# Weights of the first seven chunks decoded half a chunk at a time in one bank of PSUM

## The chip, the cores and the metric

The kernel runs on one core of a Trainium2 chip, whose engines run at the same time and each take their own instructions in order: TensorE (PE in the profile; PEld is its loading of weights), VectorE (DVE), ScalarE (ACT), GpSimd (POOL) and SyncE (SP), which here only starts transfers. A queued instruction that waits holds up whatever stands behind it on its engine. SBUF and PSUM are the two memories beside the engines; PSUM has eight banks of 512 fp32 columns by 128 partitions. The metric is the device time in microseconds of one execution.

## The reference, cut to what matters

All inputs come as float64. One layer of attention with a memory term is followed by two wide layers:

```
scores = q @ k.T / sqrt(D), causal;  a = softmax(scores);  local = a @ v
q_p = elu(q) + 1;  mem = (q_p @ M_prev) / (q_p @ z_prev + 1e-6)
x = sigmoid(beta) * mem + (1 - sigmoid(beta)) * local     # 4 batches x 576 tokens, 8 heads x 64 = 512 columns
x = elu(x @ w_in) @ w_out                                 # w_in 512 x 2048, w_out 2048 x 512
out = leaky(x @ w2_in) @ w2_out                           # leaky(h) = max(0.01 h, h)
```

The wide layers are computed with split operands: a number is a high part in the chip's fp32r type and a low part, number minus high part, and three matmuls stand for one product.

## The kernel before, in words

**Weights.** A wide layer's 2048 inner columns are 16 chunks. A chunk has 128 of them: a 128x512 block of `w_in` and one of `w_out`. `load_w` reads both as pairs of 32-bit words (low word `lw`, high word `hw`) into `wraw`, a tile with two buffers, and builds the fp32 number from bits, 1024 columns per instruction: ACT copies `hw` scaled by 2^-112 into the SBUF tile `wm` (L110); DVE shifts it left by three (L111), ors in the top three bits of `lw` (L112) and the sign (L115); ACT casts the result to the high part in `w` (L226, in `copy`); POOL subtracts the high part to get the low part, 512 columns at a time (L121). Other chunks than the first seven are decoded late, in the wide layers.

**Attention.** Batches are worked one after the other, each as four pairs of heads, each pair as items of 256 or 320 tokens. An item goes PE scores into a bank `sc` (L411 in batch 0, L413 and L414 later), DVE scale, mask and maximum (L416), ACT exponential (L421), POOL and DVE the reciprocal of the sums (L430, L431), POOL scaling (L436), PE transposes into a bank `tp` (L442), ACT copies (L447, L232), PE the product with the values (L509). Batch 0 takes plain fp32 matmuls and puts that product into banks `pm`; later batches use split operands and the single bank `po`, first written by the transposes of `qp_unit` (L315). Batch 0 thus never touches `po`.

**Order.** The seven chunks of the first layer (`dec`) are handed out during batch 0, one each time a planned cost has passed (`DSPAN`); the first layer's seven chunks are used from the end of batch 0 on, when `phase1_units` of a finished batch fill PE between attention items. The order on each engine is then set by a scheduler that goes by its own estimate of durations. When batch 0 is done, `close_decode` gives the tiles of decoding back.

**PSUM.** The eight banks: `pm` two, `sc` three, `tp` two, `po` one.

Of the kernel before, what the change touches and what calls it, by code (L numbers as in the profile page):

```python
# [10 lines left out]
I32 = mybir.dt.int32  # L11
AF = mybir.ActivationFunctionType
ALU = mybir.AluOpType
# [6 lines left out]
def _f(ap):  # L20
    return ap.bitcast(F32)
# [3 lines left out]
def kernel(  # L25
# [14 lines left out]
    nc = tc.nc  # L40
# [16 lines left out]
    E_GH, E_WH, E_VH, E_MS, E_V32, E_XH, E_RS, E_Y = "V", "A", "V", "P", "P", "A", "P", "A"  # L57
# [34 lines left out]
    def load_w(key, pool, src_i, src_o, f, slot):  # L92

        w = pool.tile([P, 2, 2, DM], F32R, tag=f"w{slot}", name=f"w{slot}")
        wi_tiles[key, f] = w[:, :, 0].rearrange("p t (c n) -> p t c n", c=NKC)
        wo_tiles[key, f] = w[:, :, 1]  # L100
        raw = pools["wst"].tile([P, 2, DM, 2], I32, tag="wraw", bufs=2, name="wraw")
        nc.sync.dma_start(
            raw[:, 0].rearrange("p (c n) t -> p c (n t)", c=NKC),
            src_i[:, f * 2 * P:(f + 1) * 2 * P].rearrange("(c p) n -> p c n", p=P),
        )
        nc.sync.dma_start(raw[:, 1].rearrange("p n t -> p (n t)"), src_o[f * P:(f + 1) * P, :])
        rw = raw.rearrange("p a n t -> p (a n) t")
        lw, hw = rw[:, :, 0], rw[:, :, 1]
        m = pools["wst"].tile([P, 2 * DM], I32, tag="wm", bufs=pools["nwm"], name="wm")
        nc.scalar.activation(out=_f(m), in_=_f(hw), func=AF.Copy, scale=2.0 ** -112)  # L110
        nc.vector.tensor_scalar(out=m, in0=m, scalar1=3, scalar2=None, op0=ALU.logical_shift_left)  # L111
        nc.vector.scalar_tensor_tensor(  # L112
            out=m, in0=lw, scalar=29, in1=m, op0=ALU.logical_shift_right, op1=ALU.bitwise_or
        )
        nc.vector.scalar_tensor_tensor(  # L115
            out=m, in0=hw, scalar=-(1 << 31), in1=m, op0=ALU.bitwise_and, op1=ALU.bitwise_or
        )
        t = _f(m).rearrange("p (a n) -> p a n", a=2)
        copy(E_WH, w[:, 0], t)
        for a in range(2):  # L120
            nc.gpsimd.tensor_tensor(out=w[:, 1, a], in0=t[:, a], in1=_f(w)[:, 0, a], op=ALU.subtract)  # L121
# [10 lines left out]
    def halves(n):  # L132
# [20 lines left out]
        out=mask[:, 448:576], in_=mask[:, 448:576], pattern=[[-1, 128]], compare_op=ALU.is_ge,  # L153
        fill=-1e30, base=0, channel_multiplier=1,
    )
    wst_a = tc.tile_pool(name="wst_a", bufs=1, side="left")
    pools = {"wst": wst_a.__enter__(), "nwm": 2}

    ones = []
    for par in range(NR):  # L160
# [30 lines left out]
    def bank(tag):  # L191
        return psum.tile([P, 512], F32, tag=tag, bufs=BANKS[tag], name=tag)
# [31 lines left out]
    def copy(eng, dst, src):  # L224
        if eng == "A":
            nc.scalar.copy(dst, src)  # L226
        else:
            (nc.vector if eng == "V" else nc.gpsimd).tensor_copy(dst, src)  # L228
# [476 lines left out]

    def close_decode():
        wst_a.__exit__(None, None, None)
        pools["outer"] = tc.tile_pool(name="mlpx", bufs=1, reuse_waits="tile", side="left")
        early = pools["outer"].__enter__()
        for tag in ("x", "y", "xh0", "xl0"):  # L710
            pools["own", tag] = early
        pools["own"] = tc.tile_pool(name="mlp", bufs=1, reuse_waits="tile", side="left")
        pools["mlp"] = pools["own"].__enter__()
# [17 lines left out]
    c_mlp = NFA * 24 * NT / 2.4  # L731
    rate = (c_mlp - RESERVE) / (c_att - DELAY)
    dec = [lambda f=f: load_w(0, wpa, w1i, w1o, f, f) for f in range(NFA)]
    fill = []
    credit = pos = 0.0
    for c, u, done in att:
        u()
        pos += c
        while dec and pos >= c0 * DSPAN * (NFA - len(dec)) / NFA:
            with tc.high_priority(offset=0):  # L740
                dec.pop(0)()
        if done == 0:
            close_decode()
        if done is not None:
            fill += [(pos + DELAY, c2, u2) for c2, u2 in phase1_units(done)]
        if fill and fill[0][0] <= pos:
            credit += c * rate
        while fill and fill[0][0] <= pos and fill[0][1] <= credit:
            _, c2, u2 = fill.pop(0)
            credit -= c2  # L750
            with tc.high_priority(offset=FILL_OFF):
                u2()
# [8 lines left out]


    wun = [(1, lambda f=f: load_w(0, wpb, w1i, w1o, f, f - NFA)) for f in range(NFA, NF)]
    tail = True
    merge(side, wun[:NPRE])
    wun = wun[NPRE:]
    w2 = [lambda f=f: load_w(1, wpa, w2i, w2o, f, f) for f in range(NFA)]
    w2 += [lambda f=f: load_w(1, wpb, w2i, w2o, f, f - NFA) for f in range(NFA, NF)]
    def recut(dst, scr, t0, n):
# [136 lines left out]
```

## Time and profile before

| what | value |
|---|---|
| median of 3 runs | 1123.6 us (1121.98 to 1123.76) |
| the profiled execution, its own time | 1123.19 us |
| its span in the trace | 1121.4 us |
| busy PE, PEld | 1066.8 us (95%), 917.1 us (82%) |
| busy DVE, ACT, POOL | 600.0 us, 493.9 us, 599.9 us |
| share of the chain that ended last: PE, POOL, DVE | 69%, 7%, 6% |

A busy share is a mean over stages with different limits. Batch 0's attention fills the first 126 us or so, attention with the first layer's chunks between goes on to about 560 us, and the rest is wide layers alone, where PE is busy without a break. The page's line of 40 slices of 28 us shows the first stage apart: PE 6, 9, 7, 9 tenths, POOL 8, 8, 9, 7.

### The profile page before, as it was taken

What the parts mean: (1) busy time and instruction counts of PE and PEld (TensorE: products, weight loads), DVE (VectorE), ACT (ScalarE), POOL (GpSimd) and SP (SyncE); (2) the same over time, 40 slices, a digit from 0 to 9 for tenths busy, and PEclk for the clock granted to TensorE, in tenths of its full rate; (3) what the DMA queues carried; (4) which work ended last, traced back from release to release, by engine and by line L of the source; (5) the groups of instructions that cost most, each with busy time, mean ns of one, the idle gap of its engine ahead of it and who ended that gap; (6) DMA issues with size and microseconds to landing.
All of it is one profiled execution on the core that took longest, in us unless ns stands there. A gap on an engine that the chain in (4) does not pass through costs nothing.

```text
span 1121.4 us, 17423 instructions
## 1 busy us (share of the span) xinstructions
PE 1066.8 (95%) x5904; PEld 917.1 (82%) x5904; DVE 600.0 (54%) x1363; ACT 493.9 (44%) x1191; POOL 599.9 (53%) x724
## 2 busy tenths in 40 slices
PE   6979899999989999989999999999999999999997
PEld 3657799989989999868777888988888888888886
DVE  6865887788878856646666222656221232131132
ACT  6867787687877634543544223433111111111110
POOL 8897695585658634955865324755422322322222
PEclk9989999999999999989999999999999999999999
DMA  7633443563365228552646122341100110010010
GB/s 187 183 98 89 118 102 102 119 170 92 79 145 157 61 60 260 170 171 94 194 125 200 34 67 76 117 141 63 50 26 1 23 53 1 1 38 1 1 38 19
DMA packets 145912, 104.43 MB, mean 93 GB/s; under 512 B 81440, under 2 KB 139808, under 8 KB 145824
## 3 DMA queue, kind: packets, MB, share of 16 engines
q1 hardware_dynamic: 145824, 103.33, 32.1%
q8 instruction: 47, 0.77, 0.3%
q14 instruction: 41, 0.34, 0.1%
HBM read 73.80 MB, written 25.95 MB: 89 GB/s over the span
## 4 chain that ended last, share of the span: by engine, by line
PE 69%; DMA 9%; POOL 7%; DVE 6%; ACT 4%; issue 4%; SPq 2%; DVEq 0%; POOLq 0%; ACTq 0%
PE pm L603 16%; PE sc L854 14%; PE tp L603 12%; PE sc L631 5%; PE po L854 4%; PE pm L631 4%; PE po L509 3%; PE tp L442 3%; POOL w L121 2%; DMA x<-xq 2%; PE po L631 2%; PE pm L509 2%; DMA wraw<-in_moe_w_out_dram 1%; PE sc L413 1%; PE sc L414 1%
## 5 line engine op out<-in xcount | busy, mean ns | idle before, releaser
L610 POOL TENSOR_TENSOR gl<-e,gh 128x512 fp32r<-128x512 f32 (+2 forms) x181 | 202.0, 1119 | 348.7 <-DVE gh L228 304.3
L603 PE MATMUL tp<-xw,w 128*128 128x512 f32 (+1 forms) x504 | 147.0, 374 | 5.5 <-DVE e L617 5.5
L603 PE MATMUL pm<-xw,w 128*128 128x512 f32 (+1 forms) x496 | 143.8, 371 | 0.0
L854 PE MATMUL sc<-w,gh 128*128 128x512 f32 x448 | 137.7, 393 | 0.0
L436 POOL TENSOR_SCALAR pt<-pt,rs,omg 128x128 f32<-128x128 f32 (+4 forms) x160 | 107.2, 679 | 19.4 <-DVE rs L431 15.8
L631 PE MATMUL sc<-gh,w 128*128 128x512 f32 (+2 forms) x438 | 106.8, 344 | 5.7 <-DVE gh L228 3.2
L603 PEld LDWEIGHTS tp<-xw,w 128*128 128x128 f32 x504 | 92.2, 190 | 24.3 <-DVE e L617 6.0
L121 POOL TENSOR_TENSOR w<-wm,w 128x512 fp32r<-128x512 f32 x64 | 87.5, 1387 | 37.3 <-ACT w L226 37.1
L603 PEld LDWEIGHTS pm<-xw,w 128*128 128x128 f32 x496 | 90.5, 188 | 18.4
L421 ACT ACTIVATE pt<-pt,mx 128x128 f32<-128x128 f32 (+4 forms) x160 | 93.4, 585 | 23.4 <-DVE mx L416 21.7
L854 PEld LDWEIGHTS sc<-w,gh 128*128 128x128 f32 x448 | 83.1, 188 | 17.9
L603 PE MATMUL tp<-xv,w 128*128 128x512 f32 (+1 forms) x252 | 93.9, 373 | 0.0
L603 PE MATMUL pm<-xv,w 128*128 128x512 f32 (+1 forms) x248 | 92.0, 371 | 0.0
L631 PEld LDWEIGHTS sc<-gh,w 128*128 128x128 f32 x438 | 74.3, 188 | 18.2 <-DVE gh L228 4.6
L622 ACT ACTIVATE e<-pm 128x512 f32<-128x512 f32 (+1 forms) x40 | 22.2, 554 | 151.2 <-PE pm L603 151.1
L228 DVE CAST gh<-e 128x512 fp32r<-128x512 f32 (+2 forms) x146 | 76.5, 527 | 20.4 <-PE po L631 7.5
L442 PE MATMUL tp<-ident,pt 128*128 128x128 f32 x480 | 79.3, 277 | 8.3 <-ACT ah L232 3.2
L854 PE MATMUL sc<-w,gl 128*128 128x512 f32 x224 | 85.4, 393 | 0.0
L623 DVE TENSOR_TENSOR e<-tp,e 128x512 f32<-128x512 f32 (+1 forms) x40 | 25.4, 636 | 108.1 <-ACT e L622 108.1
L623 DVE TENSOR_TENSOR e<-pm,e 128x512 f32<-128x512 f32 (+1 forms) x40 | 25.5, 636 | 106.7 <-ACT e L622 106.6
L603 PE MATMUL pm<-xh,w 128*128 128x288 f32 x368 | 80.1, 303 | 2.1 <-ACT xh L226 1.7
L416 DVE CUSTOM_DVE_ANT_0 pt<-sc,mask 128x128 f32<-128x128 f32 (+4 forms) x160 | 69.0, 448 | 12.1 <-PE tp L442 6.0
(149 smaller groups left out, 2466.6 us busy)
## 6 DMA issues: line engine op xcount, KB each, us to landing
wraw<-in_moe_w_in_dram SPq DMA_DIRECT2D x32, 512.0 KB, 4.1
wraw<-in_moe_w_out_dram SPq DMA_DIRECT2D x32, 512.0 KB, 5.2
ys<-st SPq DMA_DIRECT2D x32, 144.0 KB, 3.3
x1s<-st SPq DMA_DIRECT2D x36, 128.0 KB, 1.8
x<-x1s SPq DMA_DIRECT2D x9, 512.0 KB, 3.6
out_dram<-st SPq DMA_DIRECT2D x36, 128.0 KB, 1.7
vn<-in_v_dram SPq DMA_DIRECT2D x64, 64.0 KB, 2.4
xq<-xp SPq DMA_DIRECT2D x24, 160.0 KB, 1.9
```

Of the source, the lines that this page charges most:

```text
L121: nc.gpsimd.tensor_tensor(out=w[:, 1, a], in0=t[:, a], in1=_f(w)[:, 0, a], op=ALU.subtract)
L228: (nc.vector if eng == "V" else nc.gpsimd).tensor_copy(dst, src)
L416: nc.vector.tensor_tensor_reduce(out=pt[0:m, k0:k0 + n], in0=sc[0:m, 0:n], in1=mk, op0=ALU.add, op1=ALU.min, scale=-0.125, scalar=mx[0:m, ...
L421: nc.scalar.activation(out=pt[0:m, 0:nk], in_=pt[0:m, 0:nk], func=AF.Exp, scale=-1.0, bias=mx[0:m, last:last + 1], accum_out=self.pd["ss"] ...
L436: nc.gpsimd.tensor_scalar(out=pt, in0=pt, scalar1=rs[0:m, i:i + 1], scalar2=omg[0:m, h:h + 1], op0=ALU.mult, op1=ALU.mult,)
L442: nc.tensor.transpose(dst, self.p[c][:, k0:k0 + kn], ident)
L509: nc.tensor.matmul(po[:, a:b], w, x, start=i == 0, stop=i == len(mms) - 1)
L603: nc.tensor.matmul(ph, wi[:, wj, kc, :], xx[:, kc, :], start=n_mm == 0, stop=n_mm == 11)
L610: nc.gpsimd.tensor_tensor(out=gl, in0=g, in1=_f(gh), op=ALU.subtract)
L623: nc.vector.tensor_tensor(out=t, in0=ph, in1=t, op=ALU.max)
L631: nc.tensor.matmul(py, wo[:, wj, ec * P:(ec + 1) * P], gg, start=opens and f == first and n_mm == 0, stop=closes and f == last and n_mm == 2,)
L854: nc.tensor.matmul(pos[tb], gg[:, tb * P:(tb + 1) * P], wo[:, wj, :], start=f == 0 and n_mm == 0, stop=f == NF - 1 and n_mm == 2,)
```

## The change

For the first seven chunks a chunk is decoded as two halves, `w_in` and then `w_out`, of 512 columns. [...] There is one bank `po`, so a half begins when the half before it has been subtracted. The two tiles `wm` of the first pool go away. After batch 0 the old code runs, for all other chunks.

```diff
         nc.sync.dma_start(raw[:, 1].rearrange("p n t -> p (n t)"), src_o[f * P:(f + 1) * P, :])
+        if pools["decode_bank"]:
+            for a in range(2):
+                lw, hw = raw[:, a, :, 0], raw[:, a, :, 1]
+                t = bank(pools["decode_bank"])
+                m = t.bitcast(I32)
+                nc.scalar.activation(out=t, in_=_f(hw), func=AF.Copy, scale=2.0 ** -112)
+                nc.vector.tensor_scalar(out=m, in0=m, scalar1=3, scalar2=None, op0=ALU.logical_shift_left)
+                nc.vector.scalar_tensor_tensor(
+                    out=m, in0=lw, scalar=29, in1=m, op0=ALU.logical_shift_right, op1=ALU.bitwise_or
+                )
+                nc.vector.scalar_tensor_tensor(
+                    out=m, in0=hw, scalar=-(1 << 31), in1=m, op0=ALU.bitwise_and, op1=ALU.bitwise_or
+                )
+                copy(E_WH, w[:, 0, a], t)
+                nc.vector.tensor_tensor(out=w[:, 1, a], in0=t, in1=_f(w)[:, 0, a], op=ALU.subtract)
+            return
...
-    pools = {"wst": wst_a.__enter__(), "nwm": 2}
+    pools = {"wst": wst_a.__enter__(), "nwm": 2, "decode_bank": "po"}
...
         wst_a.__exit__(None, None, None)
+        pools["decode_bank"] = None
```

The scheduler places everything anew. On ACT, before, the first decode stands behind the exponentials of the first item (L421; `pt` is an item's scores, `w0` chunk 0):

```order
L421 ACTIVATE pt0_267,ss0_130<-pt0_267,mx_268 128x128
L421 ACTIVATE pt1_273,ss0_130<-pt1_273,mx_274 128x256
L421 ACTIVATE pt20_157,ss1_138<-pt20_157,mx_284 64x320
L110 ACTIVATE wm_194<-wraw_191 128x1024
L421 ACTIVATE pt3_289,ss1_138<-pt3_289,mx_290 128x448
L447 COPY d320_132<-tp_304 128x384
```

And after (L437 is the exponential now, L112 the first copy, L242 the cast):

```order
L437 ACTIVATE pt0_273,ss0_130<-pt0_273,mx_274 128x128
L112 ACTIVATE po_194<-wraw_191 128x512
L437 ACTIVATE pt1_279,ss0_130<-pt1_279,mx_280 128x256
L437 ACTIVATE pt20_157,ss1_138<-pt20_157,mx_290 64x320
L437 ACTIVATE pt3_295,ss1_138<-pt3_295,mx_296 128x448
L242 CAST w0_190<-po_194 128x512
```

The first copy has moved ahead of two exponentials, and the cast of the first half stands four rows behind it.

On DVE near the end of batch 0, before, where the operands of batch 1's first pair (`qs0_1233`, `qs1_1234`) are split, no decoding is left; DVE's part of it ended behind the 36th score instruction, and `pt0_1305` is the 49th, the first of batch 1:

```order
L328 TENSOR_TENSOR qs0_1233<-sc_1253,qs0_1233 64x320
L328 TENSOR_TENSOR qs1_1234<-sc_1235,qs1_1234 64x256
L431 RECIPROCAL rs_1247<-rs_1247 128x3
L416 ISA pt0_1305,mx_1306<-sc_1307,mask_118 128x128
L416 ISA mx_1306 128x1
L416 ISA pt1_1317,mx_1318<-sc_1319,mask_118 128x256
```

After, the same operands are `qs0_1275` and `qs1_1276`, the same scores `pt0_1347`, `pt1_1359` and `pt20_157` (L432), and `w6` is the seventh chunk:

```order
L344 TENSOR_TENSOR qs1_1276<-sc_1277,qs1_1276 64x256
L114 SCALAR_TENSOR_TENSOR po_1010<-wraw_1000,po_1010 128x512
L395 RECIPROCAL den_1309<-den_1309 128x10
L432 ISA pt0_1347,mx_1348<-sc_1349,mask_118 128x128
L432 ISA mx_1348 128x1
L344 TENSOR_TENSOR qs1_1276<-sc_1295,qs1_1276 64x320
L117 SCALAR_TENSOR_TENSOR po_1010<-wraw_1000,po_1010 128x512
L432 ISA pt1_1359,mx_1360<-sc_1361,mask_118 128x256
L432 ISA mx_1360 128x1
L432 ISA pt20_157,mx_1390<-sc_1391,mask_118 64x320
L432 ISA mx_1390 64x1
L121 TENSOR_TENSOR w6_999<-po_1010,w6_999 128x512
```

The last half of the last chunk now stands between these splits, and its subtraction (L121) behind the scores `pt20_157`. By the count of score instructions ahead of it, a half is finished every three to four scores, from the 7th to the 51st; before, the seven chunks were finished between the 9th and the 36th.

## Rows read from the trace of the kernel before

**Rows 1.** Windows by stage: length, busy per engine (instructions), PEclk, DMA share, GB/s.

```profile
38.00:64.00 26.00, 21.96 (x109) 15.53 (x107) 19.44 (x45) 20.83 (x50) 25.02 (x27) 1.00 0.64 191
64.00:77.00 13.00, 7.91 (x41) 5.50 (x40) 11.40 (x18) 8.43 (x20) 12.51 (x12) 0.94 0.34 98
77.00:96.00 19.00, 17.72 (x78) 13.39 (x79) 7.41 (x29) 12.23 (x34) 15.75 (x29) 0.86 0.32 72
96.00:112.00 16.00, 15.84 (x94) 13.62 (x93) 10.90 (x40) 13.87 (x41) 12.32 (x19) 1.00 0.36 82
112.00:126.00 14.00, 12.97 (x84) 10.52 (x83) 12.67 (x37) 11.79 (x33) 9.35 (x15) 1.00 0.46 105
126.00:560.00 434.00, 410.08 (x2802) 383.69 (x2801) 318.67 (x797) 280.92 (x740) 284.21 (x381) 0.98 0.47 131
```

**Rows 2.** Chain that ended last, 36 to 78 us: shares, then start, us, what.

```profile
by line: POOL w L121 29.5%; POOL pt L436 19.8%; issue 12.7%; ACT pt L421 5.2%; PE tp L442 3.8%; DVE wm L112 3.6%; POOL ph_e L374 3.6%; POOL m L342 3.4%; POOL rs L430 3.2%; POOL ph_e L381 3.0%; ACT wm L110 2.7%; PE pm L509 2.3%; PE sc L411 1
...
46.93 6.12 POOL pt L436 x5
...
64.10 4.22 POOL w L121 x2
...
68.34 1.12 ACT wm L110
...
73.22 2.24 POOL w L121
75.46 1.57 POOL pt L436
...
77.08 0.69 PE tp L442 x2
```

**Rows 3.** Groups by form, 0 to 90 us: busy us, mean ns.

```profile
L436 POOL TENSOR_SCALAR pt<-pt,rs,omg 128x448 f32<-128x448 f32 x6 | 5.9, 990 | 0.0
```

**Rows 4.** The same group, 130 to 560 us.

```profile
L436 POOL TENSOR_SCALAR pt<-pt,rs,omg 128x448 f32<-128x448 f32 x22 | 16.0, 726 | 0.0
```

**Rows 5.** Groups of decoding by form, 0 to 130 us.

```profile
L121 POOL TENSOR_TENSOR w<-wm,w 128x512 fp32r<-128x512 f32 x14 | 21.3, 1539 | 0.5 <-ACT w L226 0.2
...
L115 DVE SCALAR_TENSOR_TENSOR wm<-wraw,wm 128x1024 int32<-128x1024 int32 x7 | 11.7, 1672 | 0.1
...
L112 DVE SCALAR_TENSOR_TENSOR wm<-wraw,wm 128x1024 int32<-128x1024 int32 x7 | 10.4, 1487 | 0.1
...
L111 DVE TENSOR_SCALAR wm<-wm 128x1024 int32<-128x1024 int32 x7 | 8.1, 1159 | 6.9 <-ACT wm L110 6.9
...
L110 ACT ACTIVATE wm<-wraw 128x1024 f32<-128x1024 f32 x7 | 8.1, 1153 | 3.0 <-DMA wraw<-in_moe_w_out_dram 2.9
...
L226 ACT CAST w<-wm 128x1024 fp32r<-128x1024 f32 x7 | 7.3, 1044 | 6.5 <-DVE wm L115 6.5
```

**Rows 6.** Instructions on tile wm, 0 to 135 us: shortest, median, longest ns.

```profile
L111 DVE TENSOR_SCALAR wm<-wm x7: 690/873/1765, 13.5 to 70.1; 128x1024 int32<-128x1024 int32 x7
```

**Rows 7.** Groups by form, whole span, DVE.

```profile
L623 DVE TENSOR_TENSOR e<-pm,e 128x512 f32<-128x512 f32 x32 | 22.1, 690 | 94.3 <-ACT e L622 94.3
...
L617 DVE SCALAR_TENSOR_TENSOR e<-e,pm 128x512 f32<-128x512 f32 x18 | 12.3, 682 | 32.4 <-ACT e L616 32.4
```

**Rows 8.** Groups by form, whole span, ACT.

```profile
L622 ACT ACTIVATE e<-pm 128x512 f32<-128x512 f32 x32 | 19.1, 597 | 125.9 <-PE pm L603 125.8
```

**Rows 9.** Waits of ACT and of DVE, 0 to 126 us: us in total, times, longest.

```profile
ACT w L226 <- DVE wm L115: 6.5, 4, 2.6
```

**Rows 10.** Instructions on tile po, 100 to 130 us.

```profile
L315 PE MATMUL po<-ident,ph_e x5: 272/272/273, 112.8 to 117.0; 128*128 128x128 f32 x5
```

**Rows 11.** Timeline of DVE: start, us, engine, line.

```profile
105.90 0.48 DVE L416 CUSTOM_DVE_ANT_0 pt<-sc,mask 64x320 f32<-64x320 f32 x1
```

## The prediction

> **What bounds the kernel now.** I read the stages first, as windows of the trace, because the shares of the whole span hide them. From 126 us to 560 us PE is busy 410 of 434 us, and the rest of the span is wide layers without a break; nothing there is touched but the order. What the change touches lies in batch 0, and there the reader is to see three things in [rows 1]. From 38 to 64 us POOL is busy 25.02 of 26 us and PE lacks 4.04 us. From 64 to 77 us POOL is busy 12.51 of 13 us and PE lacks 5.09 us. From 77 us on PE hardly waits (17.72 of 19 us, then 15.84 of 16 us).
>
> The chain of waits says the same of 36 to 78 us [rows 2]: POOL's subtraction of the low part (L121) is 29.5% of these 42 us, 12.4 us, and its scaling of the scores (L436) 19.8%, 8.3 us. At 64.10 us two subtractions hold the chain for 4.22 us, at 73.22 us another for 2.24 us, and the scaling that PE's transposes at 77.08 us need stands behind them. So this stage is bound by POOL, with decoding as the largest part of it.
>
> [...]
>
> **The change part by part.** *POOL loses* the 14 subtractions, 21.3 us [rows 5]. It also gets faster at what is left: the scaling of 128x448 takes 990 ns on the mean before 90 us and 726 ns later [rows 3, 4], when far less decoding is about. I put this down to DVE's decoding, which before works on SBUF alone. [...]
>
> *DVE* loses L111, L112 and L115 of 1024 columns, 8.1 + 10.4 + 11.7 = 30.2 us [rows 5], and gets 14 x 4 instructions of 512 columns. None with a result in PSUM is in the trace. Nearest are those with one operand in PSUM and 512 columns, 690 and 682 ns [rows 7]; the lower bound is half the shortest L111 of 1024 columns, 345 ns [rows 6], and a bound above is the 1159 ns that a disturbed L111 takes in the mean. I take 0.69: 56 x 0.69 = 38.6 us, 8.4 us more than before (by the bounds 11 us less to 35 us more, the upper one only if the contention stayed). [...] By the SBUF pace the 14 shifts would be 14 x 0.345 = 4.8 us cheaper, 0.7 us of it in term D.
>
> *ACT* loses 8.1 + 7.3 = 15.4 us [rows 5]. The cast from PSUM is like L622, 597 ns [rows 8]; the copy into PSUM has no row, and lies between half of L110, 577 ns, and the whole, 1153 ns. I take 0.60 for each: 14 x 1.20 = 16.8 us, 1.4 us more (1.0 to 9).
>
> *SP* issues the same 14 loads; the third chunk's now stand behind the loads of the next pair's values, which delays decoding and nothing that attention reads. The two tiles that go free were used by decoding alone.
>
> *The wait that is added* is the single bank. A half takes 0.60 + 3 x 0.69 + 0.60 + 0.69 = 3.96 us in series, and four hand-overs between ACT and DVE. Queued behind ACT's cast are exponentials, which POOL and then PE wait for; behind DVE's shift are score maxima, which ACT waits for. PE's transposes into `po`, at 112.8 us before [rows 10], must wait for the last subtraction; it stands behind a score that was at 105.90 us [rows 11], so they need not, if the order holds.
>
> Terms on the path, each with its bounds:
>
> - A, 38 to 64 us. Of the 12.4 us of L121 some 5.5 us lie here (12.4 less 4.22, 2.24 and a piece of 0.44), and 1.6 us of scaling go with the contention. But ACT is busy 20.83 of 26 us and PE 21.96, so PE's 4.04 us are all there is to win, and the round of ACT, DVE and PE is late next: 1.5 us (0 to 4).
> - B, 64 to 77 us. 4.22 + 0.44 + 2.24 us of L121 and 1.12 us of L110 leave the chain. PE lacks 5.09 us; ACT and DVE have room only because the decoding is spread over a longer time: 4.0 us (2 to 5).
> - C, the clock. PE's busy time at less than the full clock costs 17.72 x 0.14 + 7.91 x 0.06 = 3.0 us. If PE does not idle in B it is not lost: 2.0 us (0 to 3).
> - D, 96 to 112 us. Two halves now lie here, 2.4 us of ACT and 5.5 us of DVE. ACT has 16 - 13.87 = 2.1 us free and DVE 5.1, PE nothing: they will be late, by 2.5 us (0 to 8). The two halves between 77 and 96 us are hidden, where DVE has 11.6 us and ACT 6.8 us free.
>
> Sum: -1.5 - 4.0 - 2.0 + 2.5 = -5.0 us on the profiled execution's own 1123.2 us (span 1121.4 and 1.8 us around it), 0.4 us below the median. PE is the bound after 126 us, so it is carried to the end: 1118.5 us, about 5 us below the median.
>
> **The rivals.**
>
> *The hand-overs between ACT and DVE become the bound; slower.* Before, ACT's cast waits 6.5 us for DVE [rows 9] and L111 6.9 us for ACT [rows 5], 13.4 us in seven chunks of two such waits each. After, there are 14 halves with four hand-overs, twice to four times as many. For it speaks that a queue cannot go round the instruction that waits; against it that the half-sized steps are each half as long and the scheduler put other work between. If the waits double, ACT has 13 us more of them, and it is idle in only 21 of the 88 us of batch 0 in [rows 1]; about 10 us of these would land on the round that now bounds A, B and D, against 5 us won: 1128 us. It decides once a half takes over 7 us, for then 14 of them pass the 112.8 us at which `po` is wanted.
>
> *No change.* ACT and PE are each over 80% busy in A, and full in D. If A gives nothing, B half and D 4 us, the sum is -2.0 - 1.0 + 4 = +1: 1123.5 us.
>
> *More than forecast.* All of PE's idle time in A and B goes and the clock with it, and D is hidden: 4 + 5 + 3 = 12 us, 1111.5 us. Against it: PE's own start of an item needs the maximum and exponential ahead of it.
>
> *The order after 126 us.* Every engine's order differs up to the wide layers. PE lacks 24 us from 126 to 560 us, so a transfer earlier or later there may move the time by 3 us either way; this is width, not a case of its own.
>
> **How the numbers follow.** The forecast, 1113 to 1121 us, has a chance of 0.57; more than forecast 0.08; no change 0.15; slower 0.20. A measurement of this kernel can tell some 0.2%, 2.2 us, from no change. Faster by more is then 0.65, within it 0.15, slower by more 0.20. The range reaches into the slower case: 1111 to 1128 us.
>
> **What would show it right or wrong.** In the profile after: POOL about 25 us less busy before 112 us; the scaling of 128x448 near 730 ns; PE's idle time from 38 to 77 us halved, and its clock near 1.00 from 64 to 96 us; DVE's in-place instructions near 0.69 us; no wait of PE for `po` on DVE's L121. Wrong would be: ACT's casts waiting for L117 by more than 10 us in all, PE idle between 96 and 112 us for longer than 5 us, or the end of batch 0 no earlier than before.

## The result, and the profile after

The change takes the kernel from 1123.43 us to 1110.45 us, the medians of eight runs each on one chip; one of the eight after took 1118.83 us, the others 1108.55 to 1112.5. The ratio, with its 95% interval, is 0.9892 [0.9874, 0.9911], a little nearer to 1 than that of the medians: 12 us by the ratio, 13 by the medians, where 5 were forecast. The median lies 0.55 us below the lower end of the range, 1111 us. The profiled execution took 1110.38 us, its span is 1108.6 us, so 1.8 us lie around the span as before.

The stages of the kernel after, as windows with the columns of [rows 1] (the first row and the last are new; the last reaches past the end):

```profile
0.00:38.00 38.00, 28.15 (x119) 18.32 (x120) 28.14 (x89) 26.05 (x71) 27.11 (x62) 1.00 0.72 189
38.00:64.00 26.00, 26.00 (x149) 21.03 (x148) 20.60 (x57) 22.99 (x64) 16.48 (x30) 1.00 0.60 168
64.00:77.00 13.00, 13.00 (x71) 10.40 (x70) 11.46 (x34) 11.48 (x32) 8.97 (x17) 1.00 0.72 187
77.00:96.00 19.00, 18.08 (x99) 13.90 (x98) 17.91 (x48) 16.93 (x47) 10.82 (x17) 1.00 0.37 85
96.00:112.00 16.00, 12.76 (x85) 10.49 (x83) 14.31 (x42) 12.85 (x37) 11.03 (x19) 1.00 0.37 85
112.00:126.00 14.00, 11.75 (x82) 9.84 (x81) 13.48 (x45) 11.28 (x36) 10.22 (x18) 1.00 0.51 138
126.00:560.00 434.00, 411.14 (x2776) 385.28 (x2775) 313.57 (x769) 277.02 (x715) 275.80 (x368) 0.98 0.47 132
560.00:1122.00 562.00, 541.38 (x2538) 447.14 (x2536) 180.59 (x319) 114.99 (x209) 203.26 (x183) 1.00 0.16 50
```

PE (the first busy column) has no gap at all from 38 to 77 us, where it lacked 4.04 and 5.09 us; POOL (the fifth) is busy 25.5 of these 39 us where it was busy 37.5; the clock is 1.00 throughout. The price stands in the fifth and sixth row: PE now lacks 3.24 and 2.25 us, and DVE (the third) is busy 27.8 of these 30 us.

The same two rows of the kernel before that [rows 1] doesn't show:

```profile
0.00:38.00 38.00, 27.32 (x119) 18.82 (x120) 26.76 (x75) 25.59 (x64) 32.15 (x58) 1.00 0.68 176
560.00:1122.00 562.00, 553.04 (x2587) 456.06 (x2585) 192.72 (x329) 120.19 (x216) 208.58 (x187) 1.00 0.17 54
```

With them PE's account is complete, since its idle and busy time fill the span: the spans differ by 12.8 us, PE's whole busy time fell by 4.6 us (1066.85 to 1062.27) and its idle time by 8.2 us. The windows are fixed in time while the kernel after runs up to 16 us ahead, so that a window does not hold the same work before and after.

The decoding after, groups by form from 0 to 115 us (busy us, mean ns | idle before, and what ended it), to stand against [rows 5]:

```profile
L114 DVE SCALAR_TENSOR_TENSOR po<-wraw,po 128x512 int32<-128x512 int32 x14 | 9.7, 695 | 0.3
L117 DVE SCALAR_TENSOR_TENSOR po<-wraw,po 128x512 int32<-128x512 int32 x14 | 9.7, 693 | 0.2
L113 DVE TENSOR_SCALAR po<-po 128x512 int32<-128x512 int32 x14 | 9.7, 692 | 3.7 <-ACT po L112 3.6
L121 DVE TENSOR_TENSOR w<-po,w 128x512 fp32r<-128x512 f32 x14 | 9.6, 687 | 3.2 <-ACT w L242 3.1
L112 ACT ACTIVATE po<-wraw 128x512 f32<-128x512 f32 x14 | 9.1, 649 | 3.1 <-DMA wraw<-in_moe_w_in_dram 3.0
L242 ACT CAST w<-po 128x512 fp32r<-128x512 f32 x14 | 8.2, 586 | 3.0 <-DVE po L117 3.0
```

Every DVE step, the subtraction (L121) now among them, takes 0.69 us, as estimated, ACT's two 0.65 and 0.59. The waits between ACT and DVE for these steps are 3.6 + 3.1 + 3.0 = 9.7 us, fewer than the 13.4 before.

POOL's scaling from 0 to 90 us, first before (the group of 128x448 is in [rows 3]), then after:

```profile
L436 POOL TENSOR_SCALAR pt<-pt,rs,omg 128x256 f32<-128x256 f32 x6 | 4.8, 807 | 0.0
L436 POOL TENSOR_SCALAR pt<-pt,rs,omg 128x128 f32<-128x128 f32 x6 | 4.1, 679 | 0.3 <-DVE rs L431 0.3
```

```profile
L452 POOL TENSOR_SCALAR pt<-pt,rs,omg 128x448 f32<-128x448 f32 x7 | 5.0, 713 | 0.0
L452 POOL TENSOR_SCALAR pt<-pt,rs,omg 128x256 f32<-128x256 f32 x8 | 4.4, 552 | 0.0
L452 POOL TENSOR_SCALAR pt<-pt,rs,omg 128x128 f32<-128x128 f32 x8 | 3.6, 446 | 3.9 <-DVE rs L447 2.9 <-DVE den L394 0.9
```

The same instructions lost about 230 to 280 ns each. Why is to be seen in the trace of the kernel before, instruction by instruction (start, us, engine, line). At 46.92 us POOL scales an item in three instructions, at 61.04 us another of the same three forms:

```profile
46.92 3.69 POOL L436 TENSOR_SCALAR pt<-pt,rs,omg 64x320 f32<-64x320 f32 x3
61.04 2.11 POOL L436 TENSOR_SCALAR pt<-pt,rs,omg 64x320 f32<-64x320 f32 x3
```

and DVE's decoding beside them:

```profile
46.98 0.74 DVE L111 TENSOR_SCALAR wm<-wm 128x1024 int32<-128x1024 int32 x1 [2.50 <-ACT wm L110]
48.08 1.22 DVE L112 SCALAR_TENSOR_TENSOR wm<-wraw,wm 128x1024 int32<-128x1024 int32 x1
62.02 1.68 DVE L111 TENSOR_SCALAR wm<-wm 128x1024 int32<-128x1024 int32 x1
```

In the first run DVE's instructions go at about their own pace (the shift 0.74 us for 0.69 at its shortest [rows 6]) and POOL takes 1.58 us longer; in the second POOL is undisturbed and DVE's shift ends 0.55 us behind POOL's run. This reads as exclusion, not as a shared bandwidth: one goes on, the other stands. Who has the turn these rows do not settle, and the last section shows a case in which the one issued first had to wait.

When the n-th of the 192 score instructions (L416 before, L432 after) starts, read from the timelines of DVE; batch 0 has 48. The last two columns are kernels of the next section:

| n | before | after | or-steps on two SBUF operands | bank, but POOL subtracts |
|---|---|---|---|---|
| 29 | 57.45 | 51.20 | 52.36 | 52.11 |
| 45 | 95.56 | 79.34 | 82.65 | 80.86 |
| 49 | 102.77 | 92.60 | 96.43 | 88.00 |
| 65 | 127.08 | 115.51 | 119.90 | 115.38 |
| 192 | 391.14 | 380.66 | 385.82 | 378.88 |

The lead is 16.2 us at the 45th score, 10.2 at the 49th: 6 us are given back there. It is 10.5 at the 192nd; 2.3 us more are won behind it, where the change does nothing but alter the order.

### The profile page after: what moved, and what is told of

The parts are those of the page before. It is cut to its first block, busy times and chain, and to the rows that moved or that the text cites. A ratio compares the mean times of both kernels' runs of the same rounds, so it can differ in the third digit from the quotient of the medians.

```text
span 1108.6 us, 17441 instructions
## 1 busy us (share of the span) xinstructions
PE 1062.3 (96%) x5904; PEld 916.4 (83%) x5904; DVE 600.1 (54%) x1398; ACT 493.6 (45%) x1205; POOL 563.7 (51%) x710
## 4 chain that ended last, share of the span: by engine, by line
PE 69%; DMA 8%; DVE 8%; POOL 6%; issue 4%; ACT 3%; SPq 2%; DVEq 0%; POOLq 0%; ACTq 0%
PE pm L619 16%; PE sc L871 14%; PE tp L619 12%; PE sc L647 5%; PE po L871 4%; PE po L525 4%; PE pm L647 4%; PE tp L458 3%; POOL xv L806 2%; PE sc L429 2%; POOL w L137 1%; PE po L647 1%; PE sc L430 1%; DMA wraw<-in_moe_w_out_dram 1%; DMA x1s<-st 1%
## 5 line engine op out<-in xcount | busy, mean ns | idle before, releaser
L452 POOL TENSOR_SCALAR pt<-pt,rs,omg 128x128 f32<-128x128 f32 (+4 forms) x160 | 102.0, 646 | 19.6 <-DVE rs L447 18.1
L437 ACT ACTIVATE pt<-pt,mx 128x128 f32<-128x128 f32 (+4 forms) x160 | 93.3, 584 | 24.9 <-DVE mx L432 23.4
L871 PEld LDWEIGHTS sc<-w,gh 128*128 128x128 f32 x448 | 83.1, 188 | 17.9
L458 PE MATMUL tp<-ident,pt 128*128 128x128 f32 x480 | 81.7, 276 | 5.4 <-DVE dl L251 2.0
L639 DVE TENSOR_TENSOR e<-tp,e 128x512 f32<-128x512 f32 (+1 forms) x40 | 25.5, 636 | 107.7 <-ACT e L638 107.6
L639 DVE TENSOR_TENSOR e<-pm,e 128x512 f32<-128x512 f32 (+1 forms) x40 | 25.5, 637 | 106.9 <-ACT e L638 106.9
L137 POOL TENSOR_TENSOR w<-wm,w 128x512 fp32r<-128x512 f32 x50 | 66.2, 1343 | 30.1 <-ACT w L242 30.1
L638 ACT ACTIVATE e<-tp 128x512 f32<-128x512 f32 (+1 forms) x40 | 22.1, 553 | 117.4 <-PE tp L619 117.2
```

Source lines behind the costliest of these rows:

```text
L437: nc.scalar.activation(out=pt[0:m, 0:nk], in_=pt[0:m, 0:nk], func=AF.Exp, scale=-1.0, bias=mx[0:m, last:last + 1], accum_out=self.pd["ss"] ...
L452: nc.gpsimd.tensor_scalar(out=pt, in0=pt, scalar1=rs[0:m, i:i + 1], scalar2=omg[0:m, h:h + 1], op0=ALU.mult, op1=ALU.mult,)
L458: nc.tensor.transpose(dst, self.p[c][:, k0:k0 + kn], ident)
L638: nc.scalar.mul(t, ph, 0.01)
L639: nc.vector.tensor_tensor(out=t, in0=ph, in1=t, op=ALU.max)
L871: nc.tensor.matmul(pos[tb], gg[:, tb * P:(tb + 1) * P], wo[:, wj, :], start=f == 0 and n_mm == 0, stop=f == NF - 1 and n_mm == 2,)
```

## The experiments

Diffs are against the changed kernel unless said otherwise. "Before" was run beside each, so that kernels of different rows are compared by their ratios; a difference of two ratios has an uncertainty of some 3 us.

| kernel | median us | ratio to before, 95% |
|---|---|---|
| half chunks in an SBUF tile, DVE subtracts | 1121.15 | 0.9981 [0.9962, 1.0001] |
| half chunks in SBUF tiles, POOL subtracts | 1121.19 | 0.997 [0.9956, 0.9985] |
| before, but DVE subtracts | 1125.85 | 1.0038 [1.0016, 1.006] |
| bank, last or-step to SBUF, POOL subtracts | 1111.84 | 0.9908 [0.988, 0.9936] |
| one extra two-operand DVE step, early | 1125.11 | 1.0012 [0.9995, 1.0028] |
| one extra shift out of the bank | 1116.81 | 0.994 [0.9922, 0.9958] |
| or-steps on two SBUF operands | 1114.52 | 0.9924 [0.9901, 0.9947] |
| extra subtraction, two SBUF operands | 1120.13 | 0.9977 [0.9961, 0.9993] |
| extra subtraction, bank and w | 1115.01 | 0.993 [0.9913, 0.9948] |
| extra subtraction, bank and hw | 1117.90 | 0.9936 [0.9913, 0.9959] |
| or-steps and extra on two SBUF operands | 1126.94 | 1.0031 [1.0015, 1.0046] |
| DSPAN 0.6 | 1110.87 | 0.9896 [0.986, 0.9932] |
| last three chunks: POOL subtracts | 1119.28 | 0.9964 [0.9947, 0.9981] |
| after, RESERVE 58000 | 1114.65 | 0.9913 [0.989, 0.9937] |
| before, RESERVE 58000 | 1122.63 | 0.9985 [0.9972, 0.9999] |

**The parts apart.** Three theories stood: POOL is relieved of 14 subtractions; half-sized steps let other work in between; or DVE and POOL no longer exclude each other because DVE works in PSUM. Four kernels hold the parts apart.

```
-                t = bank(pools["decode_bank"])
+                t = pools["wst"].tile([P, DM], F32, tag="wm", bufs=1, name="wm")
```

> The changed kernel with its half-chunk in an SBUF tile (one buffer) instead of the bank of PSUM; low parts still by VectorE. Relief theory (the gain is POOL's 21.3 us of subtractions gone): about 1110 us, as the changed kernel, POOL's scaling of 128x448 anywhere. Contention theory (the gain is that VectorE's decoding no longer reads two SBUF tiles): about 1119 us, the 128x448 scaling back at 900 to 1000 ns before 90 us, VectorE's or-steps over 0.8 us in the mean instead of 0.69. Step-size theory (half-sized steps hold the queues for less time): about 1111 us.

```
-                t = bank(pools["decode_bank"])
+                t = pools["wst"].tile([P, DM], F32, tag="wm", bufs=2, name="wm")
...
-                nc.vector.tensor_tensor(out=w[:, 1, a], in0=t, in1=_f(w)[:, 0, a], op=ALU.subtract)
+                nc.gpsimd.tensor_tensor(out=w[:, 1, a], in0=t, in1=_f(w)[:, 0, a], op=ALU.subtract)
```

> Half-chunks in SBUF (two buffers), low parts by POOL as before: only the size of the steps differs from the kernel before. Step-size theory: 1111 to 1114 us. Relief theory: 1121 to 1125 us, since POOL keeps its 21 us. Contention theory: 1121 to 1125 us too, the 128x448 scaling still at 900 to 1000 ns before 90 us.

Against the kernel before; `nwm` is 2 for the first seven chunks alone:

```
-            nc.gpsimd.tensor_tensor(out=w[:, 1, a], in0=t[:, a], in1=_f(w)[:, 0, a], op=ALU.subtract)
+            (nc.vector if pools["nwm"] == 2 else nc.gpsimd).tensor_tensor(
+                out=w[:, 1, a], in0=t[:, a], in1=_f(w)[:, 0, a], op=ALU.subtract
+            )
```

> The kernel before with only the low parts of the first seven chunks moved from POOL to VectorE, whole chunks, all in SBUF. Relief theory: 1111 to 1115 us. Contention theory: 1119 us or more, since VectorE has 14 more instructions with two SBUF operands. Step-size theory: 1122 us or more, since VectorE's steps of 1024 columns stay and it has 9 us more work.

```
+                s = pools["wst"].tile([P, DM], F32, tag="wm", bufs=2, name="wm")
...
-                    out=m, in0=hw, scalar=-(1 << 31), in1=m, op0=ALU.bitwise_and, op1=ALU.bitwise_or
+                    out=s.bitcast(I32), in0=hw, scalar=-(1 << 31), in1=m, op0=ALU.bitwise_and, op1=ALU.bitwise_or
...
-                copy(E_WH, w[:, 0, a], t)
-                nc.vector.tensor_tensor(out=w[:, 1, a], in0=t, in1=_f(w)[:, 0, a], op=ALU.subtract)
+                copy(E_WH, w[:, 0, a], s)
+                nc.gpsimd.tensor_tensor(out=w[:, 1, a], in0=s, in1=_f(w)[:, 0, a], op=ALU.subtract)
```

> Half-chunks built in the bank of PSUM, but the last or-step writes an SBUF tile, from which ScalarE casts and POOL subtracts: the changed kernel with POOL's subtractions back. Contention theory: 1108 to 1113 us, POOL's subtractions at 1.26 us each (17.7 us in all) and its scaling undisturbed. Relief theory: 1119 to 1123 us. Step-size theory: about 1111 us. If VectorE is the bound at the end of the changed kernel's batch 0, this run has 9.6 us less of VectorE there and its time from the 45th to the 65th score instruction is shorter by some 4 us than the changed kernel's.

Taking the subtractions off POOL alone makes the kernel 4 us slower (it also gives DVE 14 more steps with two SBUF operands), halving the steps in SBUF makes it 2 to 3 us faster, whichever engine subtracts (the interval of the first reaches to no change), and the kernel that keeps all 14 subtractions on POOL but builds the number in the bank has nearly the whole gain. Groups of POOL from 0 to 90 us, in the half-sized SBUF kernel with DVE's subtractions, then in the one with the bank and POOL's:

```profile
L452 POOL TENSOR_SCALAR pt<-pt,rs,omg 128x448 f32<-128x448 f32 x7 | 7.0, 1002 | 0.0
```

```profile
L122 POOL TENSOR_TENSOR w<-wm,w 128x512 fp32r<-128x512 f32 x14 | 17.9, 1275 | 3.5 <-ACT w L243 3.0
L453 POOL TENSOR_SCALAR pt<-pt,rs,omg 128x448 f32<-128x448 f32 x8 | 5.7, 712 | 0.0
```

POOL has 17.9 us of subtractions in the second and is not slowed by DVE; in the first it has none and takes 1002 ns where 712 do. The theories of relief and of step size fall as main causes. One forecast of this kernel failed: from the 45th to the 65th score it was to be some 4 us faster than the changed one, and is 1.7 us faster. But each kernel's order differs from the others' on every engine, so this doesn't price the exclusion.

**The price at an equal order.** The first try added an or-step on two SBUF operands whose result nothing reads:

```
+                nc.vector.scalar_tensor_tensor(
+                    out=x, in0=lw, scalar=29, in1=hw, op0=ALU.logical_shift_right, op1=ALU.bitwise_or
+                )
```

> The changed kernel with one more VectorE instruction per half-chunk, 14 in all, whose result nobody reads: an or of two SBUF operands, 512 columns, about 0.7 us undisturbed. Contention by two SBUF operands: 1114 to 1119 us, several us over the same dose with an operand in PSUM, and POOL's 128x448 scaling up from 713 to over 800 ns before 90 us. If only VectorE's time counts: the same as the dose with an operand in PSUM.

It missed its aim. The scheduler put the step early, and DVE stood in order for the load (its row from 0 to 115 us); POOL's 128x448 stayed at 712 ns:

```profile
L122 DVE SCALAR_TENSOR_TENSOR extra<-wraw 128x512 int32<-128x512 int32 x14 | 10.7, 766 | 10.7 <-DMA wraw<-in_moe_w_in_dram 9.2 <-DMA wraw<-in_moe_w_out_dram 1.5
```

So did a shift of 1024 columns from SBUF to SBUF in its place, 704 ns in the mean, which waited 11.4 us (1126.44 us, 1.003 [1.0016, 1.0045]), and says as little:

```
+                nc.vector.tensor_scalar(
+                    out=x, in0=raw[:, a].rearrange("p n t -> p (n t)"), scalar1=3, scalar2=None,
...
```

> The changed kernel with one more VectorE shift per half-chunk, 14 in all, SBUF to SBUF, 1024 columns, about 0.69 us at the double pace; nobody reads the result. Contention by the fast form of the shift: 1114 to 1119 us and POOL's scaling and copies slowed. If only two-operand reads contend: the same as the dose with an operand in PSUM.

Next, operands were changed and nothing else; the order stays the same on all engines:

```
-                    out=m, in0=lw, scalar=29, in1=m, op0=ALU.logical_shift_right, op1=ALU.bitwise_or
+                    out=m, in0=lw, scalar=29, in1=hw, op0=ALU.logical_shift_right, op1=ALU.bitwise_or
...
-                    out=m, in0=hw, scalar=-(1 << 31), in1=m, op0=ALU.bitwise_and, op1=ALU.bitwise_or
+                    out=m, in0=hw, scalar=-(1 << 31), in1=hw, op0=ALU.bitwise_and, op1=ALU.bitwise_or
```

> The changed kernel, but both or-steps of each half (L114, L117) read hw from SBUF as their second operand instead of the bank, so they read two SBUF operands; they still write the bank. The weights of the first seven chunks are then without meaning. ACT, POOL, PE and SP have the changed kernel's order word for word, and DVE too but for the 28 changed operands. Theory 1 (POOL and DVE slow each other when a DVE instruction reads two SBUF operands): the or-steps go from 0.69 us to 0.8 us or more, POOL's scaling of 128x448 before 90 us from 713 ns to 850 to 1000 ns, and the time from 1110.5 to 1115 to 1121 us. Theory 2 (the gain comes from the size of the steps and from what left POOL, whatever the memory): 0.69 us, 713 ns and 1110 to 1111.5 us, as in the changed kernel.

It is some 4 us slower than the changed kernel by the ratios (3.6, with an interval that just leaves out zero), just below what the first theory gave. The sign shows in the scores: 3.1 to 5.3 us late from the 45th to the 192nd. The groups, DVE from 0 to 115 us and POOL from 0 to 90 us:

```profile
L114 DVE SCALAR_TENSOR_TENSOR po<-wraw 128x512 int32<-128x512 int32 x14 | 13.1, 938 | 0.3
L117 DVE SCALAR_TENSOR_TENSOR po<-wraw 128x512 int32<-128x512 int32 x14 | 10.5, 749 | 0.1
```

```profile
L452 POOL TENSOR_SCALAR pt<-pt,rs,omg 128x256 f32<-128x256 f32 x8 | 7.0, 878 | 0.0
L452 POOL TENSOR_SCALAR pt<-pt,rs,omg 128x448 f32<-128x448 f32 x7 | 5.0, 712 | 0.0
```

The form named in the expectation, 128x448, was missed by all of DVE's steps; 128x256 was hit, 878 for 552 ns. One form's mean is a poor gauge where seven instructions are met or not by chance. Single instructions say more, POOL and then DVE:

```profile
36.50 2.12 POOL L452 TENSOR_SCALAR pt<-pt,rs,omg 64x320 f32<-64x320 f32 x3 [0.63 <-DVE rs L447]
38.70 0.53 POOL L446 TENSOR_SCALAR rs<-ss 128x2 f32<-128x2 f32 x1
```

```profile
37.28 1.87 DVE L114 SCALAR_TENSOR_TENSOR po<-wraw 128x512 int32<-128x512 int32 x1
```

The or-step is ready inside POOL's run, which ends at 38.62 us, and ends 0.53 us behind it, at 39.15. The shortest or-steps here take 0.67 and 0.69 us, as on the bank, so that two SBUF operands show no price where POOL is out of the way.

The third form of the test is an extra subtraction of 512 columns right before that of the low part, with the result unread, and with the order again equal but for the 14 rows. Three choices of operands: high part and `hw`, both SBUF; the bank and the high part; the bank and `hw`.

```
+                x = pools["wst"].tile([P, DM], F32, tag="extra", bufs=1, name="extra")
+                nc.vector.tensor_tensor(out=x, in0=_f(w)[:, 0, a], in1=_f(hw), op=ALU.subtract)
```

> The changed kernel with one more DVE subtraction of 512 columns a half whose result nothing reads: its two operands are the high part in w and hw, both SBUF. It stands right before the subtraction of the low part, so that it waits for nothing that this doesn't wait for. To be compared with the same dose with one operand in the bank (below), whose order is the same on every engine but for the 14 rows. Theory 1 (contention of two-SBUF reads with POOL): 128x448 on POOL 750 to 850 ns before 90 us, the extra instruction over 0.75 us, and the time 2 to 5 us above its twin. Theory 2: the same as its twin within 1 us.

> The same dose, a DVE subtraction of 512 columns a half whose result nothing reads, with its first operand in the bank. It adds 14 x 0.69 = 9.7 us to DVE and no second SBUF operand. Both theories: 128x448 stays near 715 ns. If DVE is the bound behind the 45th score only, some 3 to 5 us later than the changed kernel (1114 to 1116); if DVE has room, 1110 to 1112.

> The extra subtraction with its first operand in the bank and hw as second: a closer twin of the one with two SBUF operands, since wraw is held equally long and SP's order is the same too. Theory 1 (two SBUF operands exclude POOL): extra instruction 0.69 us, and 1114 to 1116 us, some 5 us below the one of two SBUF operands. Theory 2 (the 5 us came from the buffer of loads, held longer): 1119 to 1121 us.

By the ratios the two-operand form is 4.6 us over the bank and `hw` (0.9977 less 0.9936, of 1123.7), within the first theory's range; the medians, taken on two chips, are 2.2 us apart, and the 1117.90 us of the bank and `hw` lie between the ranges of its two theories. The kernel with the bank and the high part, whose loads SP issues in a slightly different order, is 5.3 us below the two-operand form. A fourth choice was run ahead of these as the control of the two doses that missed their aim: a shift out of the bank, one operand and none in SBUF.

```
+                nc.vector.tensor_scalar(out=x, in0=m, scalar1=3, scalar2=None, op0=ALU.logical_shift_left)
```

> The control of the two doses: one more shift per half-chunk, 14 in all, from the bank of PSUM to SBUF, 512 columns, about 0.69 us; nobody reads the result. VectorE has 9.7 us more to do in batch 0. If VectorE is the bound behind the 45th score instruction: 1112 to 1115 us, 2 to 4 us over the changed kernel; if it has room: 1110 to 1111 us. POOL's scaling stays near 713 ns.

It took 1116.81 us, more than either case gave; POOL's 128x448 stayed at 710 ns. Its order on ACT, DVE, POOL and PE turned out to be that of the three above, so it is one more twin: 4.2 us below the two-operand form. In that form POOL's 128x448 takes 792 ns for 707 with the bank and `hw`, and the 14 extra subtractions 15.5 us for 9.7. Then both edits together, the or-steps with `in1=hw` and the extra subtraction of two SBUF operands:

> The extra subtraction of two SBUF operands, and both or-steps reading hw from SBUF as second operand as well (meaningless weights for the first seven chunks): 42 DVE instructions of 512 columns with two SBUF operands. All engines have the order of the kernel with the extra subtraction alone, which took 1120.1 us; the or-steps alone cost 4 us on top of the changed kernel. If the prices of excluding each other add up: 1123 to 1126 us, the gain of the change gone with the number and size of DVE's instructions unchanged. If they overlap, DVE waiting once for both: 1120 to 1122 us.

The prices add up: 1.0031 against 0.9936 is 10.7 us, give or take 3, and 9.0 by the medians, between two kernels with the same instructions, counts and order, apart from which memory 42 DVE instructions read. The traces say where: the 49th score is 11.2 us later, the 192nd 10.7, so all of it arises in batch 0, and the 42 instructions take 39.2 us of DVE for 29.0. (The weights are meaningless here; the mean granted clock of the runs is 0.986 against 0.985.) Windows (columns as above), first with the bank and `hw`, then with the 42:

```profile
38.00:64.00 26.00, 26.00 (x146) 21.28 (x145) 21.66 (x61) 23.25 (x66) 18.55 (x36) 1.00 0.49 139
```

```profile
38.00:64.00 26.00, 23.15 (x114) 17.11 (x112) 21.68 (x46) 17.90 (x49) 14.73 (x21) 0.93 0.46 133
```

PE's gaps are back and the clock dips to 0.93. From 38 to 64 us DVE is as busy as in its twin with fewer instructions, 46 for 61, and POOL does 21 instructions in 14.73 us where the twin does 36 in 18.55. No engine is full: DVE and POOL stand in each other's way, and what they lose counts as busy.

**What holds the kernel now.** Does the planned pace of the chunks or the single bank set the decoding?

```
-    DSPAN = 0.75
+    DSPAN = 0.6
```

> The changed kernel with the seven chunks handed out over 0.6 of batch 0's planned cost instead of 0.75, so that decoding ends earlier. If the last two halves among batch 1's first splits cost the 5 to 6 us that the changed kernel loses between the 45th and the 49th score instruction: 1105 to 1108 us. If the single bank sets the pace of the decoding anyway: no difference, 1109 to 1112 us.

No difference, and the last subtraction starts at 96.8 us instead of 94.8 us. But the order on ACT, DVE, POOL and PE is the changed kernel's, instruction for instruction; only transfers move on SP. So the first case, decoding that ends earlier, was not put to the test. That the single bank sets the pace is argued from the changed kernel: of the 13 halves behind the first, 12 start within 1.1 us of the subtraction before them. The 45th score is 2 us later than in the changed kernel, at this order, which says how much a difference of two traces is worth. Behind the 49th score the chain of waits of the changed kernel is DVE alone for over nine microseconds, from 99.91 us (start, us, what):

```profile
100.20 1.53 DVE vv L244
101.73 0.37 DVE dl L251
102.11 0.61 DVE pt L432
102.73 0.33 DVE kl L303
...
103.13 0.39 DVE kl L303
103.52 0.40 DVE qpl L251
```

In the kernel with the bank and POOL's subtractions, which has 9.6 us less on DVE, the 49th score is 4.6 us earlier, and by the 65th this is gone. Its chain there:

```profile
102.60 0.42 ACT qph L251
103.03 0.64 ACT ph_e L387
103.66 0.31 ACT ah L251
...
104.00 0.37 ACT kk L302
...
104.39 0.43 ACT ah L251
```

So ACT's high parts of batch 1 seem to be late next, right behind DVE's low parts, and one would not win without the other; no run changes both. A mix of the two kernels, the first four chunks as changed, was meant to be the best:

```
+                s = pools["wst"].tile([P, DM], F32, tag="wm", bufs=2, name="wm") if f >= 4 else t
...
+                (nc.gpsimd if f >= 4 else nc.vector).tensor_tensor(
...
```

> The changed kernel for the first four chunks; the last three write the finished number from the last or-step into an SBUF tile, which ACT casts and POOL subtracts. POOL gets 6 subtractions back at a time when it is not the bound, DVE loses 6 x 0.69 = 4.1 us where it is full (76 to 124 us), and the bank is free earlier. If DVE's work sets the end of batch 0: 1107 to 1109 us. If POOL's subtractions come onto the path again or the round of ACT, DVE and PE holds anyway: 1110 to 1112 us.

It is 8 us slower than the changed kernel, against both cases. Up to the 65th score (114.62 us) it is 0.9 us ahead; it loses later (2.7 us behind at the 192nd score, the rest in the wide layers), where its work is the same and only the order differs. How much can an order behind batch 0 do?

```
-    RESERVE = 60000.0
+    RESERVE = 58000.0
```

> The changed kernel with RESERVE 58000 for 60000, a constant of the plan that sets how fast the first layer's work is handed out after batch 0. The order is the changed kernel's, word for word, up to about the 90th score instruction, and another behind it; the work is the same. The mixed kernel was as fast as the changed one to the 65th score and 9 us slower at the end, which raises the question how much the order behind batch 0 alone moves the time. If it moves it little (the estimate of the prediction: 3 us either way): 1107.5 to 1113.5 us. If the mixed kernel's loss is of this kind: beyond that, up to 1120 us.

> The same constant in the kernel before, whose order is unchanged up to about the 100th score instruction. Same question: within 3 us of 1123.5, or beyond. Together with its twin it says how much of a difference of two kernels with different orders can be the order behind batch 0.

By the ratios +2.4 us and -1.7 us: within the 3 us of the prediction, though the first, of four runs, is uncertain by 3 us itself, and its median lies 1.15 us above the range named. Some 3 us is the width to be given to every comparison of kernels with different orders, the first four above and the change itself too. It doesn't cover the mix's 8 us, which stay open. No kernel beat the changed one.

## Why the prediction was wrong in size

The sign and the stage were right: POOL's part in batch 0 bound the kernel, PE's gaps there went, and the clock stayed up. The sum failed in its terms, worked out from the windows as idle before and after:

| term | forecast (bounds) | measured |
|---|---|---|
| A, PE's gaps 38 to 64 us | -1.5 (0 to 4 won) | -4.0 (4.04 to 0) |
| B, 64 to 77 us | -4.0 (2 to 5 won) | -5.1 (5.09 to 0) |
| C, PE's busy time by the clock | -2.0 (0 to 3 won) | -4.6 over the whole span, some 3.0 of it by the clock from 64 to 96 us |
| D, 96 to 112 us | +2.5 (0 to 8) | +3.1 (0.16 to 3.24) |
| 112 to 126 us | none | +1.2 (1.03 to 2.25) |
| 0 to 38 and 77 to 96 us | none | -1.2 |
| behind 126 us | 3 either way | -2.2 |
| sum | -5.0 | -12.8 |

**The step that failed** is A: "ACT is busy 20.83 of 26 us and PE 21.96, so ... the round of ACT, DVE and PE is late next: 1.5 us". A busy share of 80% was read as nearly full. After, ACT is busy 22.99 and PE 26.00 of 26 us: the round had the room, since what it had waited for was POOL. The same discount was taken on B and C. Of the 7.8 us between forecast and profile, 2.5 are A's, 1.1 B's and about 1.0 C's; 1.6 more of PE's busy time stood in no term, and 2.2 behind 126 us are inside the width of 3 given for the order; the cause of both stays open. The clock that C goes by is in windows of 2 us of the kernel before 1.00 up to 74 us, 0.85 to 76, 0.50 to 82, 0.94 to 84 and 1.00 again; that PE's idle time in B lowers it was the author's estimate, and with 4.04 us idle from 38 to 64 us it stayed at 1.00. After, with no gap from 38 to 77 us, it is 1.00. D takes 0.6 off, and the two rows with no forecast cancel.

**The size under it** was the exclusion. It was priced once, on POOL's side of A, at 1.6 us, an estimate (27% of 6.12 us [rows 2], from 990 and 726 ns [rows 3, 4]), and at nothing on DVE's side. No run shows these 1.6 us as a term; what the traces show works in both directions, and on more of POOL's scaling than the form that was priced (128x256 took 807 ns before and 552 after, 128x128 679 and 446). The trace of the kernel before has its marks: 1.58 us in three instructions of POOL, and a shift of 1.68 for 0.69 us; against the shortest of each form (0.69, 1.22 and 1.21 us) DVE's 21 steps lost 8.4 us there, an estimate from [rows 5]. At an equal order 42 such instructions cost some 10.7 us. The forecast explained the gain by the 21.3 us that POOL is rid of; the kernel that keeps those on POOL has nearly the whole gain all the same, and the one that takes them off POOL but stays in SBUF has 2 us of it. So of the two mechanisms named, the one put second was the main one. The rival "more than forecast", at 0.08, came true in A, B and C and failed on D. That its 1111.5 us came so near is luck: D's 3.1 us are made up by the 3.8 us of busy time and of the order behind 126 us that it did not have either.

**D** had nearly the right size by luck, from other work than was named. No half of a chunk lies between 96 and 112 us: the last runs from 88.8 to 95.5 us, since the whole stage moved forward. DVE is full there with the low parts of batch 1 (`vv`, `dl`, `kl` in the chain above), which moved forward too.

**Right as written:** 0.69 us for DVE in PSUM, 38.7 us in all for 38.6; ACT's two steps, 1.24 us for 1.20; 128x448 at 713 ns for 730; POOL 23.3 us less busy before 112 us for 25; ACT's casts waiting 3.0 us for L117, not over 10; and no wait for `po`, with the last subtraction at 94.8 us, two microseconds ahead of PE's first transposes into it:

```profile
L121 DVE TENSOR_TENSOR w<-po,w x14: 674/691/693, 14.2 to 94.8; 128x512 fp32r<-128x512 f32 x14
L331 PE MATMUL po<-ident,ph_e x10: 270/272/273, 97.0 to 125.4; 128*128 128x128 f32 x10
```

Those transposes were at 112.8 us before [rows 10]. The rival of the hand-overs falls: over 14 halves from 9.5 to 95.5 us one takes 6.1 us, under the 7 from which it would have decided. The transposes come 15.8 us earlier and the last half only just misses them; the prediction measured the margin against the old 112.8 us.

**Wrong as written:** "PE idle between 96 and 112 us for longer than 5 us" would have been a sign against it; it is 3.24 us. That the idle time from 38 to 77 us is "halved" was too little: it is gone. The sum of "no change", +1 us, is 1124.2 us on the profiled execution, not 1123.5.

## What to carry to other kernels

Where two engines are both well below full in a stage that still has gaps, look for single instructions far above the shortest of their form and lay the other engine's timeline beside them: the excess may be a price, as it was here on both engines (1.58 us in three instructions of POOL, 1.68 for 0.69 us in a shift of DVE), and moving one operand to the other memory may remove it without moving any work, as it did here (29.0 us for 39.2 in 42 instructions of DVE). Price what comes free in a stage from all the idle time there, and then ask by name which engine is full when it is gone; a mean share of 80% was not full here (ACT's 20.83 of 26 us became 22.99). Compare memories or operands at an equal order where it can be had, and look whether the order really changed: one planning constant here left it as it was on four engines, another moved the kernel by some 2 us through the order alone.

## What was not expected of the hardware

In one place DVE, issued while POOL was busy, waited not for one POOL instruction but through several in a row: 3.38 us for a subtraction that takes 0.69 in its twin. It is in the kernel with the extra subtraction of two SBUF operands (POOL, then DVE):

```profile
47.79 2.77 POOL L454 TENSOR_SCALAR pt<-pt,rs,omg 64x320 f32<-64x320 f32 x3 [0.76 <-DVE rs L449]
50.51 0.28 POOL L360 COPY m<-mr 64x128 f32<-64x128 f32 x1
50.76 1.53 POOL L392 TENSOR_TENSOR ph_e<-ph_f,zb 128x640 f32<-128x640 f32 x1
```

```profile
49.47 3.38 DVE L122 TENSOR_TENSOR extra<-w,wraw 128x512 f32<-128x512 f32 x1
```

The subtraction is issued at 49.47 us, gets no turn between POOL's next instructions, though it was issued ahead of them, and ends at 52.85 us, 0.56 us behind the last of them. It is not always so. Earlier in the same kernel (POOL, then DVE):

```profile
21.79 1.26 POOL L399 TENSOR_TENSOR ph_e<-ph_f,den 128x640 f32<-128x640 f32 x1
23.04 1.74 POOL L454 TENSOR_SCALAR pt<-pt,rs,omg 64x320 f32<-64x320 f32 x2
```

```profile
22.48 1.12 DVE L122 TENSOR_TENSOR extra<-w,wraw 128x512 f32<-128x512 f32 x1
```

Here the subtraction ends at 23.60 us, 0.55 us behind the first POOL instruction, while the first of POOL's next ones, back to back with it, is held up: it takes 1.04 us where the same form took 0.60 at 61.04 us in the kernel before. What gives DVE its turn the runs don't show. And DVE's in-place steps on a bank, integer shifts and ors, took 673 to 711 ns per 512 columns in all 42 of the changed kernel, with POOL busy beside 34 of them.
